# K transposes by the DMA crossbar, chunk extremes by halving, and one more copy on VectorE in a sparse-attention and gated-MLP kernel

## The chip, the cores and the metric

The kernel runs on one core of a Trainium2 chip. The metric is device time in microseconds (us). A quoted median is that of all executions of a kernel (3 to 11), and a quoted range is from the fastest to the slowest. Runs e1 to e8 and e13 to e16 were on one chip, e9 to e12 on a second and e17 and e18 on a third; the kernel before was run beside each batch and took 208.5 to 208.8 us on all three. Profiles carry their own span, about 2 us shorter than the timed run.

PE is TensorE (its matmuls and its transposes), PEld its weight loads, DVE VectorE, ACT ScalarE, POOL GpSimd, SP SyncE. SBUF and PSUM are the two memories in which the program allocates its tiles; in this kernel PE writes into PSUM, and the loads land in SBUF. The granted clock is the profile's figure for the share of full speed at which PE was allowed to run. In this kernel POOL issues all loads from DRAM, and SP issues the stores and the crossbar transposes (the name used here for DMA transfers that the program writes as `dma_start_transpose` and the trace shows as DMA_TRANSPOSE).

## The reference

For 4 batches and 8 heads of 768 positions by 64, each row of q picks six chunks of 32 keys by an upper bound from the chunk's smallest and largest K. Causal softmax attention runs over the picked chunks, and the result goes through a gated MLP with a spatial projection.

```python
k_chunks = k.reshape(B, H, nc, 32, D)
k_min = np.min(k_chunks, axis=3)
k_max = np.max(k_chunks, axis=3)
ub = np.sum(np.maximum(q[:, :, :, None, :] * k_min[:, :, None], q[:, :, :, None, :] * k_max[:, :, None]), axis=-1)
top_chunks = np.argsort(np.where(causal, ub, -1e9), axis=-1)[..., -6:]
scores = np.where(selected & (pos[:, None] >= pos[None, :]), scale * q @ k.T, -1e9)
x = softmax(scores) @ v                      # heads joined: 4 x 768 x 512
h = np.maximum(x @ w_in, 0.0); u, v = halves(h)
gated = u * (w_spatial @ layer_norm(v) + b_spatial)
out = gated @ w_out
```

## The kernel before

The heads are worked in 16 pairs, four pairs to a batch.

```python
def k_transpose(self):
    if self.i < 16:                                   # always true: all K transposes are on PE
        self.kT = kT = ps_ml.tile([P, S], F16, tag="mlp", name="kTp")        # in PSUM
        for t in range(NQT):                          # six 128x128 blocks
            nc.tensor.transpose(kT[:, t * P:(t + 1) * P], self.k[:, t], identity)
    else:
        self.kT = sb.tile([P, S], F16, tag="kT", name="kT", bufs=3)          # in SBUF
        nc.sync.dma_start_transpose(out=self.kT.rearrange("d (t s) -> d t s", s=P),
                                    in_=self.k.rearrange("p t h d -> p (t h d)"))

def k_max(self):                                      # k_min likewise, with min and negate
    self.kmm = sb.tile([P, 2, NCH], F16, tag="kmm", name="kmm")
    nc.vector.tensor_reduce(self.kmm[:, 0, :], self.kT.rearrange("d (c ch) -> d c ch", ch=CHUNK),
                            axis=AX.X, op=Alu.max)

def k_operand(self, hi):                              # K half for the scores
    copy = nc.scalar.copy if self.i < 1 else nc.vector.tensor_copy
    copy(self.kh[hi][d0:d1], self.kT[d0:d1])

def a_transpose(self, hi):                            # score operand: crossbar from pair 8 on
    ...
def a_copy(self, hi):                                 # before pair 8: out of PSUM
    if self.i >= 8:
        return
    copy = nc.vector.tensor_copy if self.i < 2 and hi == 0 else nc.scalar.copy
    copy(self.a[:, :, hi, :], self.tr.rearrange("d (t s) -> d t s", s=P))

def triangle(self, hi):                               # causal mask of the diagonal blocks
    if self.b == 0:                                   # pairs 0 to 3: done by PE instead
        return
    nc.gpsimd.affine_select(out=blk, in_=blk, compare_op=Alu.is_ge, fill=0.0, ...)

def x_transpose(self):
    if 4 <= self.i < NPAIR - 1:
        nc.sync.dma_start_transpose(...)              # crossbar
    else:
        ...                                           # PE and a DVE copy
# ... cut ...
def load_k(g, hi, xy=None):                           # g: two pairs
    tiles["k", g] = sb.tile([P, 2, NQT, 2, D], F16, tag="k", name="k", bufs=3)
    nc.gpsimd.dma_start(out=..., in_=source(k, b, h, 2))
# ... cut: 14 K loads, 14 q loads of 192 KB, 8 v loads of 384 KB, and the weights, all by gpsimd
```

The softmax here doesn't subtract the row's maximum and nothing guards it: scores larger than these inputs give would overflow.

## Time and profile before

| | before |
|---|---|
| time, median of 3 | 208.53 us |
| span in the profile | 206.9 us |
| PE busy | 187.8 us, 91% |
| granted PE clock | 1.00 in every stretch |

The head of the profile page comes first. Each row of digits has 40 slices of the span, a digit being the busy share in tenths (PEclk: the granted clock in tenths).

```profile
PE 187.8 (91%) x1922; PEld 115.1 (56%) x1922; DVE 154.5 (75%) x454; ACT 158.1 (76%) x326; POOL 80.5 (39%) x100
PE   0368999898899999999999999999999999999992
DVE  6467979989799989899797999887647456365520
PEclk9999999999999999999999999999999999999999
GB/s 38 92 118 154 140 178 158 173 177 167 177 162 162 97 119 128 135 130 147 149 278 153 180 62 57 127 88 158 181 166 65 38 29 92 187 152 3 72 128 256
```

The table by stretches of the kernel before has, for each stretch, the busy time of the engines (with instruction counts), the granted clock, the DMA share and GB/s:

```profile
20.00:80.00 60.00, 55.78 (x767) 39.98 (x766) 55.03 (x175) 54.56 (x116) 41.71 (x52) 1.00 2.13 154
80.00:140.00 60.00, 60.00 (x632) 36.40 (x631) 53.61 (x159) 48.68 (x107) 15.21 (x16) 1.00 1.19 136
```

Two stages can be read there. From 80 us on PE is full. From 20 to 80 us PE, DVE and ACT are all at 90% or so; the DMA traffic runs at 140 to 178 GB/s by slices up to 67 us and at 97 to 128 from there to 80. The chain of waits is mostly PE work, with hardly any DMA:

```profile
PE 69%; ACT 17%; DVE 8%; issue 2%; DMA 2%; POOL 0%; DVEq 0%; ACTq 0%; POOLq 0%
```

These are the groups the change touches: the two reduces, the K operand copy, and the K transposes on PE. The columns are busy time, mean ns of one, and idle time before.

```profile
L194 DVE COPY kh<-kTp 64x768 f16<-64x768 f16 x30 | 16.5, 549 | 0.5
L178 DVE TENSOR_REDUCE kmm<-kTp 128x24 f16<-128x768 f16 x16 | 15.2, 948 | 3.7 <-PE kTp L170 2.7 <-ACT e L271 0.7
L182 DVE TENSOR_REDUCE kmm<-kTp 128x24 f16<-128x768 f16 x16 | 15.1, 945 | 0.0
L170 PE MATMUL kTp<-identity,k 128*128 128x128 f16 x96 | 8.8, 230 | 5.9 <-DMA k<-in_k_dram 5.7
```

Last, the DMA issues, with the median time from issue to landing in the last column:

```profile
k<-in_k_dram POOLq DMA_DIRECT2D x14, 192.0 KB, 8.1
ws_raw<-in_moe_w_spatial_dram POOLq DMA_DIRECT2D x6, 192.0 KB, 6.9
xT<-x SPq DMA_TRANSPOSE x11, 4.2
```

I read that a load that takes 8.1 us stands in a queue of other loads.

### The profile page before, as it was taken

What the parts mean: (1) busy time and instruction counts of PE and PEld (TensorE: products, weight loads), DVE (VectorE), ACT (ScalarE), POOL (GpSimd) and SP (SyncE); (2) the same over time, 40 slices, a digit from 0 to 9 for tenths busy, and PEclk for the clock granted to TensorE, in tenths of its full rate; (3) what the DMA queues carried; (4) which work ended last, traced back from release to release, by engine and by line L of the source; (5) the groups of instructions that cost most, each with busy time, mean ns of one, the idle gap of its engine ahead of it and who ended that gap; (6) DMA issues with size and microseconds to landing.
All of it is one profiled execution on the core that took longest, in us unless ns stands there. A gap on an engine that the chain in (4) does not pass through costs nothing.

```text
span 206.9 us, 5068 instructions
## 1 busy us (share of the span) xinstructions
PE 187.8 (91%) x1922; PEld 115.1 (56%) x1922; DVE 154.5 (75%) x454; ACT 158.1 (76%) x326; POOL 80.5 (39%) x100
## 2 busy tenths in 40 slices
PE   0368999898899999999999999999999999999992
PEld 0266776775666665656655656565555454444440
DVE  6467979989799989899797999887647456365520
ACT  4797989899998889785989996669999830666042
POOL 7997659596992463236114111111111110000000
PEclk9999999999999999999999999999999999999999
DMA  5999999999999999979998926648782124540356
GB/s 38 92 118 154 140 178 158 173 177 167 177 162 162 97 119 128 135 130 147 149 278 153 180 62 57 127 88 158 181 166 65 38 29 92 187 152 3 72 128 256
DMA packets 114424, 27.27 MB, mean 132 GB/s; under 512 B 109536, under 2 KB 110816, under 8 KB 114400
## 3 DMA queue, kind: packets, MB, share of 16 engines
q0 software_dynamic: 76544, 12.20, 89.8%
q1 hardware_dynamic: 37856, 14.75, 36.4%
q8 instruction: 15, 0.25, 0.5%
q14 instruction: 9, 0.07, 0.1%
HBM read 24.38 MB, written 6.29 MB: 148 GB/s over the span
## 4 chain that ended last, share of the span: by engine, by line
PE 69%; ACT 17%; DVE 8%; issue 2%; DMA 2%; POOL 0%; DVEq 0%; ACTq 0%; POOLq 0%
PE mlp L388 40%; PE sc L266 12%; ACT e L271 10%; PE acc L289 7%; PE kTp L170 2%; ACT a L257 2%; DVE kmm L178 2%; PE ub L222 2%; DMA k<-in_k_dram 2%; PE trm L251 2%; ACT vraw L398 1%; PE tr L205 1%; DVE vn L412 1%; DVE kmm L182 1%; ACT u L420 1%
## 5 line engine op out<-in xcount | busy, mean ns | idle before, releaser
L271 ACT ACTIVATE e<-sc 128x512 f16<-128x512 f32 x192 | 96.9, 553 | 14.8 <-PE sc L266 13.4
L266 PE MATMUL sc<-a,kh 128*128 128x512 f16 (+3 forms) x256 | 65.5, 308 | 2.1 <-ACT e L271 1.5
L388 PE MATMUL mlp<-w_in_sb,xT 128*128 128x512 f16 x192 | 53.0, 379 | 0.1
L278 POOL TENSOR_SCALAR_AFFINE_SELECT e<-e 128x768 f16<-128x768 f16 x24 | 20.9, 869 | 66.3 <-ACT e L271 66.3
L289 PEld LDWEIGHTS <-e 128*128 128x128 f16 x672 | 31.4, 97 | 17.0 <-DVE x L297 3.8
L388 PE MATMUL mlp<-vn,wsT 128*128 128x512 f16 x144 | 37.3, 379 | 0.0
L289 PE MATMUL acc<-vt,e 128*128 128x65 f16 x672 | 35.3, 193 | 0.7 <-DVE x L297 0.4
L266 PEld LDWEIGHTS <-kh 128*128 128x128 f16 x256 | 22.7, 98 | 13.3 <-issue 0.8
L437 ACT COPY o<-mlp 128x512 f32<-128x512 f32 x24 | 14.1, 586 | 19.5 <-PE mlp L388 19.1
L400 DVE BATCH_NORM_STATS2 stats<-vraw 128x6 f32<-128x512 f32 x24 | 16.6, 693 | 12.9 <-ACT vraw L398 12.5
L388 PE MATMUL mlp<-w_out_sb,gT 128*128 128x512 f16 x96 | 25.1, 379 | 0.0
L388 PEld LDWEIGHTS <-xT 128*128 128x128 f16 x192 | 17.2, 97 | 12.6 <-issue 0.4
L427 DVE SCALAR_TENSOR_TENSOR g<-mlp,b_col,u 128x512 f16<-128x512 f32 x24 | 17.9, 748 | 7.3 <-PE mlp L388 6.2
L232 DVE MAX8 max<-ub 128x8 f32<-128x8 f32 (+4 forms) x160 | 15.6, 165 | 5.1 <-PE ub L222 4.9
L388 PEld LDWEIGHTS <-wsT 128*128 128x128 f16 x144 | 12.9, 98 | 10.4
L178 DVE TENSOR_REDUCE kmm<-kTp 128x24 f16<-128x768 f16 x16 | 15.2, 948 | 3.7 <-PE kTp L170 2.7
L297 DVE TENSOR_TENSOR x<-acc,rec 128x384 f16<-128x384 f32 x32 | 17.6, 551 | 0.4
L336 POOL DMA_DIRECT2D qs<-in_q_dram x14 | 14.6, 1049 | 5.9 <-PE sc L266 5.9
L194 DVE COPY kh<-kTp 64x768 f16<-64x768 f16 x30 | 16.5, 549 | 0.5
L398 ACT ACTIVATE vraw<-mlp 128x512 f32<-128x512 f32 x24 | 14.4, 601 | 3.0 <-PE mlp L388 3.0
L420 ACT ACTIVATE u<-mlp 128x512 f16<-128x512 f32 x24 | 14.3, 598 | 1.7 <-PE mlp L388 1.5
L327 POOL DMA_DIRECT2D k<-in_k_dram x14 | 14.4, 1045 | 2.5 <-PE kTp L170 1.8
(67 smaller groups left out, 230.2 us busy)
## 6 DMA issues: line engine op xcount, KB each, us to landing
out_dram<-o SPq DMA_DIRECT2D x24, 256.0 KB, 2.3
vt<-in_v_dram POOLq DMA_DIRECT2D x8, 384.0 KB, 8.8
k<-in_k_dram POOLq DMA_DIRECT2D x14, 192.0 KB, 8.1
qs<-in_q_dram POOLq DMA_DIRECT2D x14, 192.0 KB, 7.5
ws_raw<-in_moe_w_spatial_dram POOLq DMA_DIRECT2D x6, 192.0 KB, 6.9
w_in_sb<-in_moe_w_in_dram POOLq DMA_DIRECT2D x8, 128.0 KB, 6.9
w_out_sb<-in_moe_w_out_dram POOLq DMA_DIRECT2D x4, 128.0 KB, 7.9
k<-in_k_dram POOLq DMA_DIRECT2D x4, 96.0 KB, 3.4
```

The source lines that it names most:

```text
L178: nc.vector.tensor_reduce(self.kmm[:, 0, :], self.kT.rearrange("d (c ch) -> d c ch", ch=CHUNK), axis=AX.X, op=Alu.max)
L194: copy(self.kh[hi][d0:d1], self.kT[d0:d1])
L266: mm(sc[:, col:col + n], lhsT=self.kh[hi][:, t * P:(t + 1) * P], rhs=self.a[:, q0 // P:(q0 + n) // P, hi, :], start=True, stop=not diag)
L271: nc.scalar.activation(out=self.e[hi][:, g * 512:g * 512 + width], in_=sc[:, 0:width], func=Act.Exp, scale=scale)
L278: nc.gpsimd.affine_select(out=blk, in_=blk, compare_op=Alu.is_ge, fill=0.0, base=0, channel_multiplier=-1, pattern=[[0, NQT], [1, P]])
L289: mm(self.av[:, qi, :], lhsT=self.e[hi][:, c:c + P], rhs=self.v[hi][:, t, 0:D + 1], start=first and n == 0, stop=last and n == len(blocks) ...
L297: nc.vector.tensor_tensor(self.x16[:, :, hi, :], in0=self.av[:, :, 0:D], in1=rec.to_broadcast([P, NQT, D]), op=Alu.mult)
L388: mm(st[group][:, 0:cols], lhsT=lhsT, rhs=rhs, start=(j == 0), stop=(j == n - 1))
L398: nc.scalar.activation(st["vraw"][:, ti, :], h, func=Act.Relu)
L400: nc.vector.bn_stats(stats, st["vraw"][:, ti, :])
L420: nc.scalar.activation(st["u"][:, ti, :], h, func=Act.Relu)
L427: nc.vector.scalar_tensor_tensor(g, in0=vs, scalar=b_col[:, ti:ti + 1], in1=st["u"][:, ti, :], op0=Alu.add, op1=Alu.mult)
```

## The change

The intent was to take 84 transposes off PE, to let DVE read K from SBUF rather than PSUM, to find the extremes with two-operand max and min (expected to take less time than a reduce), and to relieve ACT early by giving one of two operand copies to DVE up to pair 5.

```diff
         def k_transpose(self):
-            if self.i < 16:
+            if self.i < 2:
@@
         def k_max(self):
             self.kmm = sb.tile([P, 2, NCH], F16, tag="kmm", name="kmm")
-            nc.vector.tensor_reduce(self.kmm[:, 0, :], self.kT.rearrange(...), axis=AX.X, op=Alu.max)
+            self.k_bound(0, Alu.max)
+
+        def k_bound(self, m, op):
+            src = self.kT.rearrange("d (c ch) -> d c ch", ch=CHUNK)
+            if self.i >= 2:
+                for n in (16, 8):
+                    half = sb.tile([P, NCH, n], F16, tag=f"half{n}", name=f"half{n}")
+                    nc.vector.tensor_tensor(half, in0=src[:, :, 0:n], in1=src[:, :, n:2 * n], op=op)
+                    src = half
+            nc.vector.tensor_reduce(self.kmm[:, m, :], src, axis=AX.X, op=op, negate=(m == 1))
 
         def k_min(self):
-            nc.vector.tensor_reduce(self.kmm[:, 1, :], ..., op=Alu.min, negate=True)
+            self.k_bound(1, Alu.min)
@@
-            copy = nc.vector.tensor_copy if self.i < 2 and hi == 0 else nc.scalar.copy
+            copy = nc.vector.tensor_copy if self.i < 6 and hi == 0 else nc.scalar.copy
```

More of the change, by code (lines that the diff above doesn't have):

```diff
@@ L177, in k_max @@
             self.kmm = sb.tile([P, 2, NCH], F16, tag="kmm", name="kmm")
-            nc.vector.tensor_reduce(self.kmm[:, 0, :], self.kT.rearrange("d (c ch) -> d c ch", ch=CHUNK),
-                                    axis=AX.X, op=Alu.max)
+            self.k_bound(0, Alu.max)
[7 more added lines that the diff above has]
+            nc.vector.tensor_reduce(self.kmm[:, m, :], src, axis=AX.X, op=op, negate=(m == 1))
         def k_min(self):
-            nc.vector.tensor_reduce(self.kmm[:, 1, :], self.kT.rearrange("d (c ch) -> d c ch", ch=CHUNK),
-                                    axis=AX.X, op=Alu.min, negate=True)
+            self.k_bound(1, Alu.min)
         def k_bounds(self):
```

## The prediction

> **What bounds the kernel now.** Two stages. From about 77 us to the end (203) it is PE: the table by stretches gives PE 10.00 of every 10 us from 80 to 160, and in the tail the chain of waits holds 146 MLP matmuls in 31.53 us (0.216 us each). From 20 to 77 us the load is mixed: over 20 to 80, PE 55.8, DVE 55.0, ACT 54.6 of 60 us busy, the chain hopping between engines. From gaps between matmul starts I estimate 10 us of PE stall there. Loads issued between 10 and 62 us land 6 to 10 us later.
>
> **What the change moves** (14 pairs, 2 to 15).
> - PE: 84 K transposes go. In the timeline six take 0.33 us (94.35 to the next start, 94.68), so 4.6 us in all; pairs 9 to 15 (2.3 us) lie in the PE-bound stage.
> - PSUM: the K transpose leaves the three-buffer MLP pool, which should ease early stalls.
> - DVE: a reduce over 768 from PSUM takes 0.95 us. Instead: two fp16 halvings (384, 192 outputs) and a reduce over 192. [...] copies for pairs 2 to 5 add 4 x 0.55 = 2.2.
> - ACT: loses four copies of 0.80 us, 3.2 us, all before 55 us.
> - SP and DMA: 14 more crossbar transposes, each the size of today's xT ones: 1.2 us of SP issue, landing 2.7 us later when quiet but 6.9 and 8.8 under load (those issued at 72.1 and 60.9). [...]
>
> **On the critical path.** Gain: 2.3 us in the PE-bound stage; 4 to 5 us from relief of ACT, DVE and PSUM before 77 us. Loss: pair 2's K lands at 18.6 us and PE transposes it at 18.9; by crossbar it arrives about 25 to 27. Pair 2's first extreme started at 19.97, its scores at 30.2, with some 4 us slack, so 2 to 4 us are lost, more if the waiting reduce blocks work behind it on DVE. Later pairs have 3 to 10 us between K landing and use. In 85 to 105 us SP issues almost without pause, and one score-operand transpose lands 0.2 us before its matmul: up to 1 us lost there.
>
> **Predicted: 205.0 us, range 201.5 to 208.8** (8 in 10). Faster by over 2%: 0.40; within 2%: 0.55; slower: 0.05.
>
> **What would show it.** DVE busy down 12 to 14 us, ACT about 3[...]; PE still full from about 75 us; a DVE wait of some us on the K transpose near 20 to 27 us; the start of the full-PE stage 1 to 3 us earlier; K transposes landing 6 to 9 us early, 3 to 5 later.
>
> **What would make it wrong.** Slower: DVE blocked by late transposes for several pairs, or score operands late in the PE-bound stage. Faster: K transposes landing in 3 us despite load.

The cut sum came to 1.1 us of DVE time less per pair, 15.7 us in all; less the 2.2 us that stand, this is the "12 to 14 us" of DVE, and the "4 to 5 us from relief" rests on it in part. On the critical path the forecast's sum was 6.3 to 7.3 us of gain and 2 to 5 us of loss; the author put it at 205.0 us, 3.5 below the 208.5 of the kernel before.

## More of the kernel before

One load of K serves half of the heads of two pairs. The loads go through a ring of three slots, in POOL's program order, which POOL shares with the triangle masks of pairs 4 to 15 and with some small copies.

## The result, and the profile after

| | before | after |
|---|---|---|
| time, median (4 runs each) | 208.56 us | 234.53 us (233.06 to 235.92) |
| ratio | | 1.124, interval 1.119 to 1.129 |
| span | 206.9 us | 232.2 us |
| PE busy | 187.8 us | 189.6 us |
| PE idle (span less busy) | 19.1 us | 42.6 us |
| mean granted clock | 1.00 | 0.947 |

A ratio here is the mean time of one kernel's runs over the mean time of the other's in the same rounds, so it is not quite the ratio of the quoted medians. Executions over 1.5% slower than the fastest of the same kernel are left out of the means. The change made the kernel slower by 12%. Of the 25.3 us of span, 23.5 us are new PE idle time and 1.8 us are more PE busy time, although 84 of PE's 1922 instructions went. The head of the page after:

```profile
PE 189.6 (82%) x1838; PEld 112.9 (49%) x1838; DVE 151.7 (65%) x514; ACT 156.5 (67%) x322; POOL 81.0 (35%) x100
PE   0474398990797959798997399999999999999993
DVE  5482489970597959899974867676664737357430
PEclk9999599999599999799999689999999999999999
GB/s 44 91 135 152 127 121 118 148 160 106 124 159 160 139 163 156 153 156 166 147 122 228 216 78 121 95 102 104 114 169 199 43 37 45 109 207 48 45 100 261
```

The PE row has holes where it had 8s and 9s. At or near the larger holes the clock row shows two 5s and a 6. GB/s in the fifth to seventh slice fell from 140, 178, 158 to 127, 121, 118. (The slices are 5.2 us wide before and 5.8 after; over the same stretch, 20 to 40 us, it fell from 162 to 126.) More data should have been moved there, and less was. The same stretches as before:

```profile
20.00:80.00 60.00, 44.05 (x586) 31.87 (x587) 41.11 (x169) 40.94 (x87) 31.60 (x42) 0.89 2.04 138
80.00:140.00 60.00, 49.41 (x494) 28.67 (x493) 47.29 (x162) 41.05 (x91) 21.33 (x21) 0.91 1.50 157
```

PE has 11.7 us less work done between 20 and 80 us, and 10.6 us less between 80 and 140, where it had been full. DVE and ACT fell along with it, so none of the three is the new limit. The chain of waits names another, DMA:

```profile
PE 50%; DMA 22%; DVE 12%; POOL 5%; ACT 5%; issue 4%; POOLq 0%; DVEq 0%; SPq 0%
```

DMA rose from 2% to 22% of the span, of which the K transposes have 14%. The list of waits shows who waited for what (total us, times, longest us):

```profile
ACT e L278 <- PE sc L273: 34.3, 39, 7.7
DVE half L185 <- DMA kT<-k: 19.5, 4, 7.5
PE acc L296 <- DVE x L304: 14.5, 7, 7.1
```

Only four waits of DVE on a transposed K make 19.5 us (6.9, 7.5, 3.7 and 1.4). The timeline shows the two longest; the columns are start, duration, engine, line and operation, and in brackets the idle time before and its releaser. First pair 2:

```profile
18.51 2.76 SPq L173 DMA_TRANSPOSE kT<-k  x2
26.15 0.36 DVE L185 TENSOR_TENSOR half<-kT 128x384 f16<-128x384 f16 x1 [6.93 <-DMA kT<-k]
26.42 0.40 DVE L244 TENSOR_TENSOR qs<-ub,max 128x240 f16<-128x240 f32 x1
26.88 0.93 PE L258 MATMUL trm<-identity,qs 128*128 128x128 f16 x7 [4.02 <-DVE qs L244]
```

And one of the second batch:

```profile
58.75 0.36 DVE L185 TENSOR_TENSOR half<-kT 128x384 f16<-128x384 f16 x1 [7.51 <-DMA kT<-k]
59.02 0.55 DVE L304 TENSOR_TENSOR x<-acc,rec 128x384 f16<-128x384 f32 x1
59.63 1.00 PE L296 MATMUL acc<-vt,e 128*128 128x65 f16 x15 [7.14 <-DVE x L304]
```

The pattern is the same in both. (The third and fourth wait come before a PE gap of 3.9 us at 131 us, the hole beside the 6 of the clock row.) A halving that nobody needs yet stands first in DVE's order and waits for the crossbar. The next DVE instruction (a select of pair 1, a normalisation) had its data, and PE waits for that one. In the issues it can be seen that the loads are late too:

```profile
k<-in_k_dram POOLq DMA_DIRECT2D x14, 192.0 KB, 10.0
ws_raw<-in_moe_w_spatial_dram POOLq DMA_DIRECT2D x6, 192.0 KB, 12.0
kT<-k SPq DMA_TRANSPOSE x14, 7.9
```

And the groups that answer to those of before:

```profile
L201 DVE COPY kh<-kT 64x768 f16<-64x768 f16 x28 | 12.5, 445 | 0.5
L187 DVE TENSOR_REDUCE kmm<-half 128x24 f16<-128x192 f16 x28 | 9.5, 341 | 0.0
L185 DVE TENSOR_TENSOR half<-kT 128x384 f16<-128x384 f16 x28 | 9.1, 344 | 19.5 <-DMA kT<-k 19.5
L185 DVE TENSOR_TENSOR half<-half 128x192 f16<-128x192 f16 x28 | 8.4, 310 | 0.1
```

The three groups of an extreme sum to 27.0 us for 28 extremes, 0.96 us each, as much as the single reduce (0.95). Their records overlap at the edges, though. From the start of one instruction to the start of the next, where no idle time lies between, the medians are 0.27, 0.17 and 0.26 us, 0.70 together, against 0.87 for the reduce. So each extreme gained about 0.17 us, 5 us over all 28, while DVE lost far more by waiting.

### The profile page after: what moved, and what is told of

Read it like the earlier page. It is cut to its first block, busy times and chain, and to the rows that moved or that the text cites. A ratio compares the mean times of both kernels' runs of the same rounds, so it can differ in the third digit from the quotient of the medians.

```text
span 232.2 us, 4994 instructions
## 1 busy us (share of the span) xinstructions
PE 189.6 (82%) x1838; PEld 112.9 (49%) x1838; DVE 151.7 (65%) x514; ACT 156.5 (67%) x322; POOL 81.0 (35%) x100
## 3 DMA queue, kind: packets, MB, share of 16 engines
q1 hardware_dynamic: 49056, 17.51, 42.0%
## 4 chain that ended last, share of the span: by engine, by line
PE 50%; DMA 22%; DVE 12%; POOL 5%; ACT 5%; issue 4%; POOLq 0%; DVEq 0%; SPq 0%
PE mlp L395 29%; DMA kT<-k 14%; PE sc L273 9%; PE acc L296 7%; DMA vt<-in_v_dram 5%; ACT e L278 3%; DMA k<-in_k_dram 3%; DVE vn L419 2%; DVE x L304 2%; DVE kh L201 1%; POOL k L336 1%; DVE half L185 1%; POOL qs L345 1%; PE trm L258 1%; DVE max L239 1%
## 5 line engine op out<-in xcount | busy, mean ns | idle before, releaser
L278 ACT ACTIVATE e<-sc 128x512 f16<-128x512 f32 x192 | 97.8, 548 | 37.9 <-PE sc L273 34.3
L273 PE MATMUL sc<-a,kh 128*128 128x512 f16 (+3 forms) x256 | 68.8, 321 | 2.3 <-DMA a<-qs 1.3
L395 PE MATMUL mlp<-w_in_sb,xT 128*128 128x512 f16 x192 | 54.6, 385 | 0.0
L296 PE MATMUL acc<-vt,e 128*128 128x65 f16 x672 | 36.9, 197 | 18.1 <-DVE x L304 14.5
L296 PEld LDWEIGHTS <-e 128*128 128x128 f16 x672 | 32.1, 100 | 37.8 <-DVE x L304 16.7
L273 PEld LDWEIGHTS <-kh 128*128 128x128 f16 x256 | 23.6, 102 | 15.6 <-issue 2.5
L395 PE MATMUL mlp<-w_out_sb,gT 128*128 128x512 f16 x96 | 26.0, 389 | 0.0
L185 DVE TENSOR_TENSOR half<-kT 128x384 f16<-128x384 f16 x28 | 9.1, 344 | 19.5 <-DMA kT<-k 19.5
L239 DVE MAX8 max<-ub 128x8 f32<-128x8 f32 (+4 forms) x160 | 16.1, 163 | 5.5 <-PE ub L229 5.5
L350 POOL DMA_DIRECT2D vt<-in_v_dram x8 | 11.6, 1449 | 15.9 <-PE sc L273 14.4
```

What stands on the lines that cost most here:

```text
L239: nc.vector.max(self.max8[:, qi - 1, hi, :], ub[:, c0:c0 + CPT * (qi + 1)])
L273: mm(sc[:, col:col + n], lhsT=self.kh[hi][:, t * P:(t + 1) * P], rhs=self.a[:, q0 // P:(q0 + n) // P, hi, :], start=True, stop=not diag)
L278: nc.scalar.activation(out=self.e[hi][:, g * 512:g * 512 + width], in_=sc[:, 0:width], func=Act.Exp, scale=scale)
L296: mm(self.av[:, qi, :], lhsT=self.e[hi][:, c:c + P], rhs=self.v[hi][:, t, 0:D + 1], start=first and n == 0, stop=last and n == len(blocks) ...
L395: mm(st[group][:, 0:cols], lhsT=lhsT, rhs=rhs, start=(j == 0), stop=(j == n - 1))
```

## The experiments

The visible waits suggest one story, that DVE waits in program order for late transposes (the DVE-wait theory). A rival says that the transposes delay the loads, so that everything waits for something late whether DVE is in the line or not (the late-load theory). Later the rival was split: does a load wait because its slot is still being read by a transpose, because more bytes cross the DMA engines, or because of the crossbar form of the transfer? The expectations use letters for the theories that stood when they were written, and the letters change their meaning from batch to batch: in e13 to e16, for example, A is the transfers themselves and B the slots. The text here uses words instead.

"Dead transposes" are crossbar transposes into a buffer that no instruction reads, added to the kernel before. The order of instructions matters, because the scheduler may move others when one line changes. Compared trace by trace, the order on PE, DVE and ACT is exactly that of the kernel before in e2, e5, e6, e7, e14, e16 and e17, that of the kernel after in e13, and that of e9 in e10. In the kernel after itself and in e1, e3, e4, e8, e9, e11, e12, e15 and e18 it changed in places, so their times hold the effect of the new order too.

### e1_other_data: the kernel after, DVE reading data that is early

```diff
-                self.kT = sb.tile([P, S], F16, tag="kT", name="kT", bufs=3)
+                self.kT = sb.tile([P, S], F16, tag="kT", name="kT", bufs=5)
                 nc.sync.dma_start_transpose(...)
+                kts[self.i] = self.kT; self.kT = kts.get(self.i - 2, k_const)   # the K of two pairs earlier
```

> The kernel after, but its extremes and key copies read data that is there early: pairs 2 and 3 read a copy of pair 1's K, pair i from 4 on reads the transposed K of pair i-2. All 14 crossbar transposes still run; the result is wrong on purpose; one copy of 0.55 us on DVE is added. Theory A (DVE waits in program order for a transpose that lands 7 to 14 us after its issue, and PE and ACT wait behind DVE): the waits of DVE on kT, 19.5 us in the profile after, vanish, and the time falls to 203 to 209 us. Theory B (the transposes' traffic and their SP issue slow the loads and the other transposes): the time stays at 225 us or more. Theory C (the new DVE operations are slow): stays at 225 or more, with PE idle behind a busy DVE.

Measured: 233.67 us (231.18 to 234.93), ratio 1.113 to before; the result is wrong. DVE's waits on kT are gone, and nothing was gained. In their place PE waits for a mask on POOL, which had stood behind a load that waited for an earlier load:

```profile
61.11 1.02 POOL L343 DMA_DIRECT2D qs<-in_q_dram  x1 [2.78 <-DMA ws_raw<-in_moe_w_spatial_dram]
62.18 0.86 POOL L285 TENSOR_SCALAR_AFFINE_SELECT e<-e 128x768 f16<-128x768 f16 x1
63.10 0.51 PE L296 MATMUL acc<-vt,e 128*128 128x65 f16 x6 [10.29 <-POOL e L285]
```

So DVE's wait is a place where the delay shows, not the sole cause. The DVE-wait theory alone falls. (A few instructions stand in another order here, but the difference to the kernel after is under 1 us.)

### e2_traffic: the kernel before with 14 dead transposes

```diff
                     nc.tensor.transpose(kT[:, t * P:(t + 1) * P], self.k[:, t], identity)
+                if self.i >= 2:
+                    dead = sb.tile([P, S], F16, tag="kT", name="kTdead", bufs=3)
+                    nc.sync.dma_start_transpose(out=dead.rearrange("d (t s) -> d t s", s=P),
+                                                in_=self.k.rearrange("p t h d -> p (t h d)"))
             else:
```

> The kernel before, with the same instruction order on PE, DVE, ACT and POOL, plus 14 crossbar transposes of K for pairs 2 to 15 into a tile that nobody reads. Theory A: 208 to 211 us, since nobody waits for them. Theory B: the traffic alone costs most of the 26 us, so 222 us or more.

Measured: 232.27 us (231.50 to 234.76), ratio 1.115. This is the central run: PE still does all its transposes and DVE still reads PSUM, nobody waits for the new data, and 23.6 of the 26 us are there, in the instruction order of the kernel before. PE's longest gap is 13.55 us, ended at 68.04 us by a POOL mask:

```profile
68.04 0.51 PE L293 MATMUL acc<-vt,e 128*128 128x65 f16 x6 [13.55 <-POOL e L282]
```

### e3_from_8 and e4_copy_only: parts of the change

e3 has the crossbar and the halvings from pair 8 on, and the copy part unchanged. e4 has the copy part alone.

```diff
-                if self.i < 2:                              # e3, in k_transpose; k_bound likewise
+                if self.i < 8:
-            copy = nc.vector.tensor_copy if self.i < 2 and hi == 0 else nc.scalar.copy    # e4
+            copy = nc.vector.tensor_copy if self.i < 6 and hi == 0 else nc.scalar.copy
```

> The kernel after, but K goes by the crossbar (with halvings) only from pair 8 on; pairs 2 to 7 keep the transposes on PE and the single reduce. In the profile of before, K of pairs 8 to 15 lands 10 us or more ahead of use. Theory A: no DVE wait over 1 us on kT, 204 to 208 us (8 x 0.33 us of PE work less). Theory B: 210 us or more, since 8 of 14 transposes are still there.

> The kernel before with only the third part of the change: DVE copies one of the two score operands up to pair 5. ACT loses 4 x 0.80 us, DVE gains 4 x 0.55 us before 55 us. All theories: within 1.5 us of before, 207 to 210 us; so not a source of the 26 us.

Measured: e3 214.04 us (213.63 to 217.47), ratio 1.025 with interval 1.023 to 1.027. e4 210.90 us, ratio 1.011 with interval 1.009 to 1.013. The copy part, with the new order that the scheduler made of it, costs 2.2 us instead of helping; how much of that is the copies and how much the order was not separated. The crossbar from pair 8 is still a loss, but a small one: about 3 us more than e4, which shares the copy part.

### e5_dead_2_5, e6_dead_6_7, e7_dead_8_15: which dead transposes cost

```diff
-                if self.i >= 2:          # e2
+                if 2 <= self.i < 6:      # e5;  e6: 6 <= self.i < 8;  e7: 8 <= self.i
```

> Before, in the same instruction order, plus four dead transposes, of pairs 2 to 5 (in the run with all 14 dead ones they were in flight from 18.6 to 39.5 us, mostly beside short q, k and v rows and the first weight loads). Theory D (the loss comes where transposes are in flight with the weight loads: there the packets per 5 us fell from over 4000 to about 1200): at most 5 us, 209 to 214. Theory E (each transpose costs the same DMA time anywhere): 4/14 of 23.6 us, 215 us.

> Before plus two dead transposes only, of pairs 6 and 7. Without the delay of the others they start near 38 us, when the last two w_in and the first w_spatial loads are in flight. Theory D: a large loss for two transposes, 8 us or more (217 us or more). Theory E: 2/14 of 23.6 us, 212 us.

> Before plus eight dead transposes, of pairs 8 to 15, from about 52 us on; only the first two meet weight loads (w_out). Theory D: 209 to 214 us. Theory E: 8/14 of 23.6 us, 222 us. The real form of this (crossbar from pair 8) took 214.0 us.

Measured: e5 217.90 us (ratio 1.040), e6 216.83 us (1.040), e7 219.13 us (1.050), before 208.63. By the ratios two transposes cost 4.0%, four 4.0%, eight 5.0% and fourteen (e2) 11.5%. The cost is not proportional to the number, and neither of the two expectations holds in all three runs: it depends on what happens to be waiting. In e6 the longest gap of PE after the start, 5.8 us at 60 us, is ended by a mask on POOL; in e7 the longest, 4.68 us at 92 us, by a late score operand on SP, the second risk that the prediction named. In e6 the two were issued at 37.6 and 38.9 us and landed at 48.6 and 51.7, and the last spatial weights landed at 62.6 us where they had landed at 56.9.

### e8_dead_mask_pe: 14 dead transposes, the masks of pairs 4 to 7 on PE

```diff
-                diag = self.b == 0 and si == 0
+                diag = self.b < 2 and si == 0
@@
         def triangle(self, hi):
-            if self.b == 0:
+            if self.b < 2:
                 return
```

> Before plus all 14 dead transposes, but the causal mask of pairs 4 to 7 comes from PE matmuls (as for pairs 0 to 3) instead of GpSimd; that costs some 2.7 us of PE. In the run with 14 dead transposes PE stood 13.6 us behind a mask on GpSimd, which stood behind a load that waited for an earlier load to land. Theory F (the delay reaches PE by GpSimd's program order, loads in front of the mask): the 13.6 us wait goes, 212 to 220 us. Theory G (the late data themselves bind: q, k, v, weights): 226 us or more, PE waiting for operands or for DVE instead.

Measured: 231.77 us (231.52 to 232.90), ratio 1.111. The mask wait of e2 is gone, and again hardly anything was gained (0.5 us, although PE has 2.7 us more work here, 195.0 against 192.3, and a partly new order). PE now waits for the spatial weights themselves: 3.75, 3.16 and 1.96 us, ended at 65.8, 69.3 and 71.5 us, each by a landing of ws_raw. So POOL's order is also only a place where the delay shows.

### e9_before_no_w and e10_dead_no_w: without the weight loads (wrong)

Both have the 18 weight loads replaced by zero fills on DVE. e9 derives from the kernel before, and e10 adds the 14 dead transposes.

```diff
-            nc.gpsimd.dma_start(out=w_in_sb[hi * D:(hi + 1) * D, j], in_=moe_w_in[r:r + D, :])
+            nc.vector.memset(w_in_sb[hi * D:(hi + 1) * D, j], 0.0)      # and likewise ws_raw, w_out_sb
```

> Before with the 18 weight loads (w_in, w_spatial, w_out) replaced by zero fills on DVE[...]; the result is wrong on purpose. It is the control for the next kernel. Before is bound by PE from 77 us on, so taking loads away should gain little: 204 to 211 us.

> The control without weight loads, in the same instruction order, plus all 14 dead crossbar transposes. Theory H (the load stream of the first 85 us is what the transposes delay; with fewer loads there is room for them): 14 transposes cost at most 12 us over the control, against 23.6 us with the weight loads. If the transposes cost what they do for another reason (SP issue, the other crossbar transposes late), they cost 20 us or more here too.

Measured: e9 219.17 us (217.49 to 220.90), e10 219.37 us (218.88 to 222.07). The control was a miss: it is slower than the kernel before. Its instructions are in another order and small stalls are spread throughout, so a part of the delay may have been hidden in them. Its pair comparison still tells something: the K loads of pairs 6 and 7 landed at 34.7 and 35.4 us in e9 and at 40.4 and 41.3 in e10, so the transposes delay the loads here too, yet the time hardly moves: by the ratios, 1.047 and 1.055, the 14 transposes cost 0.8% here. That agrees with a delay that costs only where something is about to need the data, but with this control it doesn't show it.

### e11_from_12 and e12_from_12_plain: the crossbar for pairs 12 to 15 only

```diff
-            if self.i < 16:
+            if self.i < 12:             # e12: nothing else; e11: with the halvings for these pairs
```

> The change for pairs 12 to 15 only (crossbar and halvings), and without the third part (the copies stay on ACT). Theory H: the DMA engines have room by then; the four transposes land in 3 to 8 us, ahead of use; PE has 4 x 0.33 us less to do. 206.5 to 209 us, so up to 1% faster than before. Any theory by which a transpose costs time wherever it stands: 210 us or more.

> As the one before, but with the single reduce over 768 instead of halvings. DVE is not bound after 100 us (8 to 9 of 10 us busy), so the halvings should not matter: within 0.5% of the kernel with them.

Measured: e11 220.43 us (218.91 to 221.66), e12 218.97 us (218.63 to 220.87). A gain was expected, and this was a miss: with only four pairs' transposes the loss was 10 us, over 40% of that with fourteen, and more than with eight pairs' in e3. The halvings didn't help: e11 is 0.5% slower than e12, at the edge of the noise, and in another order. e12's timeline shows a cause of its own:

```profile
76.01 1.03 POOL L327 DMA_DIRECT2D k<-in_k_dram  x1 [13.69 <-DMA kT<-k]
77.05 0.88 POOL L278 TENSOR_SCALAR_AFFINE_SELECT e<-e 128x768 f16<-128x768 f16 x1
77.98 0.51 PE L289 MATMUL acc<-vt,e 128*128 128x65 f16 x6 [7.12 <-POOL e L278]
```

A K load needed a slot of the three that a crossbar transpose still had to read. POOL stood idle for 13.7 us before it, a mask stood behind it, and PE behind the mask.

### e13_after_k8, e14_dead_k8, e15_from_12_plain_k8, e16_before_k8: eight K slots

Each is a kernel already met (after; e2; e12; before) with a K ring of eight, so no K load waits for a transpose.

```diff
-            tiles["k", g] = sb.tile([P, 2, NQT, 2, D], F16, tag="k", name="k", bufs=3)
+            tiles["k", g] = sb.tile([P, 2, NQT, 2, D], F16, tag="k", name="k", bufs=8)
```

> The kernel after with eight K slots in place of three, so that no K load waits for a crossbar transpose; the order of instructions on all engines is the same. Theory B (slot re-use behind late transposes): most of the 26 us goes, 210 to 216 us, no K load waits on a transpose. Theory A (the transfers themselves crowd the load stream): 228 to 235 us, the gaps at 20-27 us and 55-59 us stay. My own guess lies between: 220 to 228, since the DVE wait on pair 2's K at 20-27 us touches no slot.

> The kernel before with 14 dead transposes and eight K slots (232.3 with three slots). Theory B: 208 to 214. Theory A: 226 to 233. I guess 215 to 226.

> The kernel before with the crossbar for pairs 12 to 15 only, single reduces, eight K slots (219.0 with three). Here the one 7.1 us gap at 78 us was seen to follow a K load waiting 13.7 us for a transpose that read its slot. Theory B: 206.5 to 209.5, that gap gone; theory A: 215 to 219.

> Control: the kernel before with eight K slots. Its K loads do not wait for crossbar transposes, so both theories: 207.5 to 209.5 us.

Measured, with before at 208.53:

| run | three slots | eight slots |
|---|---|---|
| after | 234.53 | e13 233.33 (231.99 to 235.00) |
| 14 dead transposes | 232.27 | e14 231.37 (230.09 to 232.35) |
| crossbar for pairs 12 to 15 | 218.97 | e15 212.00 (210.19 to 212.76) |
| before | 208.56 | e16 208.61 (208.53 to 208.91) |

Slot re-use explains some 7 of the 10 us lost in e12, and its 7.1 us gap is gone in e15. It explains about 1 us of the loss of the change, which is within the noise. In the main case it is another place where the delay shows. (My own guesses for e13 and e14 were too low.) With e14 the loads wait for no transpose, and they are late all the same: the last spatial weights land at 70.4 us, against 57.7 in e16. PE's longest gap is again one before a POOL mask, 12.07 us.

### e17_dead_plain: the same 14 moves as plain copies

e17 is e14 with one line changed. Bytes, source, queue and order stay; only the crossbar form goes.

```diff
-                    nc.sync.dma_start_transpose(out=dead.rearrange("d (t s) -> d t s", s=P),
-                                                in_=self.k.rearrange("p t h d -> p (t h d)"))
+                    nc.sync.dma_start(out=dead, in_=self.k.rearrange("p t h d -> p (t h d)"))
```

> e14 (14 dead crossbar transposes, eight K slots, 231.4 us) with the dead moves as plain copies within SBUF, of the same bytes, from the same source, by the same queue, in the same order. Theory A1 (192 KB more for the engines, whatever the form): 226 to 233 us. Theory A2 (the crossbar transpose as such holds up the load stream): 208.5 to 215 us, and the loads land within 1 us of the old kernel's for each copy or better. Each K load of 192 KB lands some 0.8 us after the one before it, so I estimate a plain copy at 0.5 to 1 us of the stream, and expect 209 to 214.

Measured: 213.86 us (213.60 to 215.22), ratio 1.026 with interval 1.023 to 1.029. The plain moves cost 5.2 us, the crossbar moves 22.8 us. The two ran on different chips, but the kernel before agreed on both within 0.2 us, and a comparison of their traces shows the same order on PE, DVE, ACT, POOL and SP. The stretch from 20 to 80 us, first in e16 (no dead moves), then in e14, then in e17 (columns as before):

```profile
20.00:80.00 60.00, 55.79 (x764) 39.93 (x760) 54.91 (x175) 54.44 (x117) 41.81 (x52) 1.00 2.29 157
```

```profile
20.00:80.00 60.00, 42.98 (x600) 31.29 (x599) 41.50 (x130) 41.95 (x88) 33.95 (x45) 0.91 2.10 149
```

```profile
20.00:80.00 60.00, 52.04 (x704) 37.04 (x702) 49.76 (x156) 50.06 (x107) 40.87 (x51) 0.97 2.06 179
```

The plain copies raised the traffic to 179 GB/s. The crossbar transposes lowered it to 149, under the 157 of e16, which has none of them. The queue on which SP's added moves go (its MB rise with them from 14.75 to 17.51), of each run (packets, the pieces in which the DMA engines move data; MB; time of these packets as a share of the 16 engines' span), first e16, then e14, then e17:

```profile
q1 hardware_dynamic: 37856, 14.75, 36.5%
```

```profile
q1 hardware_dynamic: 49056, 17.51, 45.7%
```

```profile
q1 hardware_dynamic: 39872, 17.51, 39.5%
```

The bytes of e14 and e17 are the same. Over e16, a crossbar transpose of 192 KB adds 800 packets and a plain copy 144. What a move takes from the load stream can be worked out from the landing of the last spatial weights: 57.7 us in e16, 61.3 in e17 after six copies, 70.4 in e14 after six transposes, so an estimated 0.6 us for a copy and 2.1 us for a transpose. This includes loads that were issued later because earlier ones had landed later.

Two other readings bear it out. The packet times above (share times span times 16 engines, less e16's, divided by 14, the other transfers of this queue taken as unchanged) come to an estimated 33 us for a transpose and 9.6 us for a copy, which spread over 16 engines is again 2.1 and 0.6 us. (From 20 to 60 us, where this queue carries the dead moves alone, it is 38 and 12 us, so 2.4 and 0.8.) And one load shows the delay without any later issue: the q load that POOL issued at 18.5 us in all three runs, just before the first dead move, landed at 28.9 us in e16, 30.4 with two copies after it and 31.8 with two transposes, so 0.7 us for a copy and 1.4 for a transpose. In load time a transpose thus costs two to three and a half times a copy; in kernel time 22.8 against 5.2 us. That the rest comes from slack that runs out fits the late landings, but was not tested apart.

Not all of the difference in time between e14 and e17 need be the load stream. SP took 1.3 us (median) to issue a transpose and 0.5 to issue a copy, and e14 has a PE gap of 5.5 us at 107 us that was ended by a score operand standing behind the dead transposes on SP. The kernel after has no such gap beyond 1.3 us.

### e18_xT_from_7: three of the old kernel's own crossbar transposes taken away

```diff
-            if 4 <= self.i < NPAIR - 1:
+            if 7 <= self.i < NPAIR - 1:
```

> The kernel before with the x transposes of pairs 4, 5 and 6 by PE instead of by crossbar: three transposes fewer in the loaded period (those issued at 60.9, 72.1 and 82.8 us), 18 PE transposes (0.33 us for six) and three DVE copies of 0.55 us more; the scheduler orders some other instructions differently. If every transpose in the loaded period costs this kernel 1 to 2 us as the dead ones did: 204 to 207 us. If the old kernel had slack for its own: 208 to 210.

Measured: 210.20 us (209.48 to 213.13), ratio 1.006 with interval 1.004 to 1.008. The attempt to use the finding in the other direction missed. Whether the extra PE and DVE work or the new instruction order ate what the lighter load stream gave was not separated. No version found beats the kernel before.

## Why the prediction was wrong

**The step that failed** is the price of the 14 crossbar transposes. The prediction charged them 1.2 us of SP issue and a longer landing of their own, and then said "Later pairs have 3 to 10 us between K landing and use". That takes the loads as fixed in time. The runs show in its place that each transpose pushes back the loads behind it by an estimated 1.4 to 2.1 us in the loaded period, so the cushion went with every transpose. In the kernel before, K of pair 6 landed at 37.9 us and PE transposed it at 45.8, a cushion of 7.9 us; in the kernel after it landed at 47.3, and its crossbar transpose at 58.7. Dead transposes alone, whose data nobody reads, cost 23.6 us (e2), and 22.8 where no load waits for a slot of theirs either (e14). The missing term was a charge on the stream of loads. The transposes' own landing was as predicted in the median (7.9 us, against 6.9 and 8.8), though later for pair 6 (11.4).

**The other half was not asked.** The prediction read in the trace before that crossbar transposes land late beside loads (6.9 and 8.8 us, against 2.7 when quiet). It did not ask whether the loads would land late beside the transposes. From the kernel before to the kernel after, K loads go from 8.1 to 10.0 us, spatial weights from 6.9 to 12.0.

**The mechanism named as a risk was right, its size was not.** "DVE blocked by late transposes for several pairs" happened: four waits, 19.5 us. "2 to 4 us are lost" for pair 2 was close, and for the reason given: the transposed K arrived at 26.1 us ("about 25 to 27") and PE idled 4.0 us. But the risk was held to be local, and e1 shows that the wait could be removed and the delay still found PE by way of POOL. e8 shows the same for POOL's masks, e13 and e14 for the slots. Several ways led to PE, and removing any one of them gained about 1 us or less. Why the delay reached POOL can be read in the issues: in these traces each load started only after the load eight before it had landed. In e14 the q load issued at 59.3 us waited for the ws_raw load eight issues earlier, landed at 58.7:

```profile
59.27 1.02 POOL L340 DMA_DIRECT2D qs<-in_q_dram  x1 [3.46 <-DMA ws_raw<-in_moe_w_spatial_dram]
```

None of the 63 loads of e14 is an exception, and none of those in the kernels before and after and in e2. So a late landing also went with late issues of the next loads.

**Smaller terms.**
- PE: the 84 transposes went, as predicted. PE busy still rose by 1.8 us, which fits the lower clock (0.947 in the mean). Gaps of 4.0, 7.1 and 3.9 us each went with 6.8 us at half clock, and a gap of only 2.0 us (ended at 94.5 us) went with 3.4 us at half clock, while one of 2.4 us (ended at 85.7 us) went with none. The full-width score matmul took 403 ns in the mean, not 387. How much of the time lost is due to this was not tested apart.
- DVE: "busy down 12 to 14 us" was wrong; it fell 2.8 us, from 154.5 to 151.7. The times assumed for the three operations are cut from the forecast; measured from start to start they were 0.27, 0.17 and 0.26 us. The comparison was one fault: the prediction set its sum against the reduce's recorded duration, 0.95 us, instead of its own start-to-start time, 0.87. Over 28 extremes that is worth about 2 of the 10 us that are missing. The records of the three (0.34, 0.31, 0.34) sum to as much as the single reduce's.
- The operand copy's records have a mean of 0.445 and a median of 0.36 us (0.549 in the mean from PSUM, before), but from start to start it takes 0.27 where no idle time lies between. Two took 1.18 and 1.34 us, both beside a DMA issue of POOL (a v load). Nine other copies that overlap a DMA issue of POOL took 0.32 to 0.44 us, so the overlap alone does not explain the two, and no run here tests what does.
- ACT: predicted relief of about 3 us of busy time; it fell 1.6. e4 shows that the relief was no gain: moving those copies to DVE costs 2.2 us, new order included.

**What stays open.** The crossbar form, not the bytes, makes most of the loss (22.8 us in e14 against 5.2 in e17), and it comes with 800 packets where a copy has 144. By the packet times above, a transpose's packets take an estimated 41 ns each and a copy's 66 ns, so it is their number and not their length that makes the sum of a transpose larger; whether the same crossbar move in fewer packets would be cheap was not tried. Of the 17.6 us between the two, the share of SP's longer issue (one gap of 5.5 us) is not measured apart either. That no more than eight loads are in flight is only read from issues and landings; whether the program or the chip sets that number was not tried.

## What to carry to other kernels

Before moving work to a DMA transpose, look at whether the loads in that stretch already land much later than they do when quiet (here 8.1 us against 3.4 for half the size at the start). If so, price the transpose as a delay to every load behind it (here an estimated 1.4 to 2.1 us each), and test that price with dead transposes that nobody reads before rewriting anything. When removing the most visible wait gains nothing, look for a late resource upstream that reaches the bottleneck by several ways at once. And check in the traces that the control runs have the same instruction order.
